# Writing the order of three engines by hand in token passes two and three, and moving the sums of w2 in pass one

## The chip, the core and the metric

The kernel runs on one core of a Trainium2 chip. The metric is the device time of one execution, in microseconds. Five engines take part: TensorE (PE in the profile; its weight loads are PEld), VectorE (DVE), ScalarE (ACT), GpSimd (POOL) and SyncE (SP, which only issues DMAs here). Each engine works through its own queue in order and waits on semaphores for the others.

## What is computed

Block attention, a two-layer MLP, and a mixture of eight experts whose gate is balanced by eight rounds of row and column normalisation. The part that the change touches is the last loop.

```python
# attention (4 batches, 8 heads, 576 tokens, 64 wide) -> x[2304, 512]
h = x @ w_in; x = np.maximum(0.01 * h, h) @ w_out          # 512 -> 2048 -> 512
logits = x @ w_gate                                        # 8 experts
P = np.exp(logits - logits.max())
for _ in range(8):
    P /= P.sum(1, keepdims=True) + 1e-09
    P /= P.sum(0, keepdims=True) + 1e-09
    P *= N / E
out = np.zeros((N, D))
for e in range(E):                                         # E = 8
    h = np.maximum(x @ w1[e], 0.0)                         # 512 -> 1024
    out += P[:, e:e + 1] * (h @ w2[e])                     # 1024 -> 512
```

## The kernel before

All matrix products keep 32-bit accuracy by splitting each operand into a high and a low part, so one product is three matmuls: high by high, high by low, low by high. A split is a ScalarE copy (the high part) and a VectorE subtract (the low part), the helpers `halves`, `parted` and `x_step`.

The expert stage works on three token passes of 768 tokens. In a pass the work is cut into 32 groups of 256 hidden columns (8 experts by 4), which are done in pairs, so a pass has 16 **steps**. A step does `first` 14 times (seven Strassen-Winograd products for each group of the pair; `product` is 6 matmuls of 384 columns), and turns their PSUM results into the four quarters of the hidden layer.

In pass one a step then ends with six `combine` calls (72 matmuls of 512 columns). Pass one also makes the weights' parts: `w2_split` splits a raw w2 tile for this pass; `w2_more` builds four sums of its quarters on GpSimd, in place in the raw tile, splits them (`halves`) and stores the parts in DRAM through the SP queue (`keep_parts`) for the later passes. The high half goes into the tile `wb`, the low half into the tile `tl`, one after the other. `w2_load` then fetches the next raw tile into the same place.

In passes two and three all steps but the last of a pass also use Strassen-Winograd for the second matrix: the hidden quarters are gated by a row of P (`seat["row"]`, fetched by `row_load`), and for each group four sums S1 to S4 are formed on GpSimd. The seven operands S1, S3, A11, A22, S2, A12, S4 are each split by `parted`. Then `seventh(n, j, c)` multiplies operand j of both groups by its w2 part: 6 matmuls of 384 columns for each of two halves c, accumulated over the step's two groups in PSUM and added by VectorE into `seat`. Between the sevenths `first(n + 2, j)` for j below 6 does the first six products of the next step, so a step of these passes begins with eight products in a row (numbers 6 to 13), and then runs seven blocks of two sevenths. That is 14 x 6 + 14 x 6 = 168 matmuls of 384 columns in a step. PSUM gives the sevenths and two of the products four banks in turn (`o_bank`).

TensorE's order is fixed by hand (`in_order`). The order of VectorE, ScalarE, GpSimd and SP is set by a scheduler from its own estimate of times; `behind` and `tc.issue_after` bind single instructions to come later in a queue than others. In the trace most names are those of tiles that were laid out anew for the later passes: `xllate` holds the splits of S1 and S3, `xhlate` those of S2 and S4, `wraw` and `slots` those of A11 and A22, `wa`, `wb`, `slots` those of A12; `places` and `xa` hold quarters and sums, and `xa` also the seats.

These lines of `quarter_late` say which sums are issued when a quarter is done:

```python
sums = {"A22": [("S1", "A21", "A22", ALU.add)],
        "A11": [("S3", "A11", "A21", ALU.subtract), ("S2", "S1", "A11", ALU.subtract)],
        "A12": [("S4", "A12", "S2", ALU.subtract)]}
```

Of the kernel before, what the change touches and what calls it, by code (L numbers as in the profile page):

```python
# [36 lines left out]
def block_attention_mlp_moe(  # L37
# [697 lines left out]
    def w2_more(n):  # L735
        if n >= N0:
            return
        raw = w2_raw.pop(n)
# [4 lines left out]
        nc.gpsimd.tensor_tensor(out=b21, in0=b22, in1=b21, op=ALU.subtract)  # L743
        for part, x in ((0, raw[:, DM:2 * DM]), (1, raw[:, 0:DM])):
# [71 lines left out]
    def x_src(p, k, make):  # L816
# [4 lines left out]
        if make and change:  # L821
            nc.vector.tensor_tensor(out=src, in0=change[0], in1=change[1], op=ALU.subtract)
        return src

    def x_step(p, k, make=True):
        src = x_src(p, k, make)
        hi, lo = (xpart.tile([P, 2, HT], F32R, name=f"x{n}{k}", tag=f"x{n}{k}") for n in "hl")
        nc.scalar.copy(out=hi, in_=src)
        nc.vector.tensor_tensor(out=lo, in0=src, in1=f32(hi), op=ALU.subtract)
        bq[p, k] = (hi, lo)  # L830
# [101 lines left out]

    def keep_late(n, name, k):
        nc.scalar.copy(out=place[k, n % 2], in_=bank[n, name][:, 0:HT])  # L934

    def parted(n, k, x):
        hi, lo = hq[n, k] = slot[k, n % 2]
        nc.scalar.copy(out=hi, in_=x)
        nc.vector.tensor_tensor(out=lo, in0=x, in1=f32(hi), op=ALU.subtract)  # L939

    def quarter_late(n, k, name, add):
        g, x, r = n % 2, bank[n, name][:, 0:HT], ROLE[k]
        q = {j: place[j, g] for j in ("A11", "A12", "A21", "A22", "S1", "S2", "S3", "S4")}
        y = q[r]
        if add:
            nc.vector.tensor_tensor(out=y, in0=x, in1=place[add, g], op=ALU.add)  # L946
            x = y
        nc.vector.scalar_tensor_tensor(  # L948
            out=y, in0=x, scalar=0.0, in1=seat["row"][:, int(k[1]) - 1], op0=ALU.max, op1=ALU.mult
        )  # L950
        sums = {"A22": [("S1", "A21", "A22", ALU.add)],
                "A11": [("S3", "A11", "A21", ALU.subtract), ("S2", "S1", "A11", ALU.subtract)],
                "A12": [("S4", "A12", "S2", ALU.subtract)]}
        if r == "A12":
            parted(n, r, y)
        for to, i0, i1, op in sums.get(r, ()):
            nc.gpsimd.tensor_tensor(out=q[to], in0=q[i0], in1=q[i1], op=op)  # L957
            parted(n, to, q[to])
            if to in ("S1", "S3"):
                parted(n, r, y)  # L960

    def quarter_last(n, k, name, add):
        g, x, r = n % 2, bank[n, name][:, 0:HT], ROLE[k]
        if add:
            c = place[add, g]
            nc.vector.tensor_tensor(out=c, in0=x, in1=c, op=ALU.add)
            x = c
        hi, lo = hq[n, k] = slot["S2" if r == "A21" else r, g]
        nc.scalar.activation(out=hi, in_=x, func=AF.Relu)
        t = nc.vector.scalar_tensor_tensor(out=lo, in0=x, scalar=0.0, in1=f32(hi), op0=ALU.max, op1=ALU.subtract)  # L970
        last_taken[:] = [getattr(t, "ins", t)]
# [5 lines left out]
    def seventh(n, j, c):  # L977
# [10 lines left out]
        if groups[n][1:] == (0, 0):  # L988
            nc.scalar.copy(out=to, in_=o)
        else:  # L990
            nc.vector.tensor_tensor(out=to, in0=o, in1=to, op=ALU.add)  # L991
        return mm

    def join(j):
        if j == 4:
            nc.vector.tensor_tensor(out=seat[6], in0=seat[6], in1=seat[1], op=ALU.add)
            nc.vector.tensor_tensor(out=seat[7], in0=seat[7], in1=seat[6], op=ALU.add)
            nc.gpsimd.tensor_tensor(out=seat[6], in0=seat[6], in1=seat[5], op=ALU.add)
            nc.vector.tensor_tensor(out=seat["row"], in0=seat[7], in1=seat[5], op=ALU.add)
# [299 lines left out]
```

## Time and profile before

| what | value |
|---|---|
| time, median of 3 runs | 2337.99 us (2335.53 to 2339.16) |
| the profiled execution, its own time | 2337.28 us |
| its span, first to last instruction | 2335.5 us |
| PE busy | 2146.5 us (92%) |
| DVE busy | 1586.6 us (68%) |
| ACT busy | 847.2 us (36%) |
| POOL busy | 655.3 us (28%) |
| mean granted TensorE clock | 0.952 of full speed |
| DMA moved | 436.87 MB, 187 GB/s on the mean |

Attention fills the span up to 202 us, the MLP up to 586, pass one up to 1139, pass two up to about 1728, pass three the rest. The shares of busy time are averages over these stages. The chain that ended last, the idle time in front of a group of instructions and the timeline of one step say more.

### The profile page before, as it was taken

How to read it: one execution, taken by the hardware profiler on the slowest of the kernel's cores; microseconds unless marked ns; L12 is line 12 of the kernel's file. 1: busy time of each engine (PE TensorE's matmuls, PEld its weight loads, DVE VectorE, ACT ScalarE, POOL GpSimd, SP SyncE). 2: the span in 40 equal slices, each digit the busy share in tenths (PEclk: the TensorE clock that was granted, in tenths of full speed). 3: DMA queues.
4: the chain of work that ended last, by engine and by line, in shares of the span. 5: the costliest groups of instructions: out<-in, count | busy, mean ns of one | idle time of the engine just before them, and what ended most of it. 6: DMA issues, size and time to landing. Idle time of an engine off the chain costs nothing.

```text
span 2335.5 us, 31639 instructions
## 1 busy us (share of the span) xinstructions
PE 2146.5 (92%) x11196; PEld 1946.8 (83%) x11196; DVE 1586.6 (68%) x2707; ACT 847.2 (36%) x1826; POOL 655.3 (28%) x642
## 2 busy tenths in 40 slices
PE   9999999999999999999798888989898898989888
PEld 6667889888888888888787887878798787878787
DVE  7886656655686777777657667675775667576766
ACT  7775322233444444444332222222333222222222
POOL 2222212210245444444112222131312213131221
PEclk9999999999999999999898989989898988989899
DMA  5551201100578888889665656465665646555562
GB/s 138 122 126 43 64 28 46 46 28 30 210 279 299 294 302 290 301 294 331 235 219 187 221 186 223 174 218 188 224 239 185 224 170 219 191 201 209 186 226 87
DMA packets 235742, 436.87 MB, mean 187 GB/s; under 512 B 77864, under 2 KB 114728, under 8 KB 235328
## 3 DMA queue, kind: packets, MB, share of 16 engines
q1 hardware_dynamic: 234384, 434.56, 54.2%
q8 instruction: 88, 1.44, 0.2%
q14 instruction: 70, 0.57, 0.1%
q10 hardware_dynamic: 1200, 0.30, 0.1%
HBM read 308.82 MB, written 125.95 MB: 186 GB/s over the span
## 4 chain that ended last, share of the span: by engine, by line
PE 80%; DVE 15%; DMA 3%; issue 1%; ACT 0%; POOL 0%; SPq 0%; ACTq 0%; DVEq 0%; POOLq 0%
PE h_ps L842 23%; PE o L985 20%; PE o L1032 11%; PE h_ps L499 9%; PE o L519 8%; PE sc L317 3%; DVE xllate L939 3%; DVE slots L939 3%; DVE wraw L939 2%; PE av L382 2%; PE tr L357 2%; DMA k_0h<-wb 2%; DVE places L948 1%; DVE places L946 1%; DVE xa L948 1%
## 5 line engine op out<-in xcount | busy, mean ns | idle before, releaser
L991 DVE TENSOR_TENSOR xa<-o,xa 128x384 f32<-128x384 f32 x392 | 217.2, 555 | 276.4 <-PE o L985 275.4
L985 PE MATMUL o<-xllate,w2h 128*128 128x384 f32 x480 | 169.4, 419 | 165.0 <-DVE xllate L939 141.4
L957 POOL TENSOR_TENSOR xa<-xa 128x384 f32<-128x384 f32 x90 | 105.9, 1177 | 718.4 <-DVE xa L948 678.5
L985 PEld LDWEIGHTS o<-xllate,w2h 128*128 128x128 f32 x480 | 111.9, 238 | 191.9 <-DVE xllate L939 158.7
L842 PE MATMUL h_ps<-xhS,w1h 128*128 128x384 f32 x768 | 259.0, 337 | 6.7 <-ACT places L934 6.7
L842 PE MATMUL h_ps<-xlS,w1h 128*128 128x384 f32 x768 | 257.9, 336 | 0.0
L842 PE MATMUL h_ps<-xhS,w1l 128*128 128x384 f32 x768 | 257.7, 336 | 0.0
L934 ACT COPY places<-h_ps 128x384 f32<-128x384 f32 x192 | 91.9, 480 | 434.9 <-PE h_ps L842 423.9
L842 PE MATMUL h_ps<-xhA,w1h 128*128 128x384 f32 x448 | 164.5, 367 | 10.2 <-DVE c L859 9.7
L842 PE MATMUL h_ps<-xlA,w1h 128*128 128x384 f32 x448 | 162.1, 362 | 0.0
L842 PE MATMUL h_ps<-xhA,w1l 128*128 128x384 f32 x448 | 160.7, 359 | 0.0
L842 PEld LDWEIGHTS h_ps<-xhS,w1h 128*128 128x128 f32 x768 | 145.2, 189 | 7.0 <-ACT places L934 7.0
L842 PEld LDWEIGHTS h_ps<-xlS,w1h 128*128 128x128 f32 x768 | 145.2, 189 | 0.0
L842 PEld LDWEIGHTS h_ps<-xhS,w1l 128*128 128x128 f32 x768 | 145.2, 189 | 0.0
L1032 PE MATMUL o<-w2h,xhlate 128*128 128x512 f32 x408 | 143.9, 391 | 0.0
L1032 PE MATMUL o<-w2h,xllate 128*128 128x512 f32 x384 | 134.4, 390 | 0.6 <-ACT xllate L865 0.5
L985 PE MATMUL o<-xhlate,w2h 128*128 128x384 f32 x480 | 121.8, 334 | 0.0
L519 PE MATMUL o<-hh,w2h 128*128 128x512 f32 (+1 forms) x320 | 117.7, 368 | 0.0
L519 PE MATMUL o<-hh,w2l 128*128 128x512 f32 (+1 forms) x320 | 117.7, 368 | 0.0
L759 POOL TENSOR_TENSOR wa<-wraw 128x256 f32<-128x256 f32 x32 | 28.2, 881 | 318.2 <-DVE w1l L777 310.6
L507 DVE TENSOR_TENSOR g<-h_ps,g 128x512 f32<-128x512 f32 (+1 forms) x80 | 50.9, 636 | 97.1 <-ACT g L506 96.8
L519 PE MATMUL o<-hl,w2h 128*128 128x512 f32 (+1 forms) x320 | 115.2, 368 | 0.0
(259 smaller groups left out, 5738.2 us busy)
## 6 DMA issues: line engine op xcount, KB each, us to landing
wraw<-in_moe_w_dram SPq DMA_DIRECT2D x64, 512.0 KB, 4.6
w1h<-k_1h SPq DMA_DIRECT2D x64, 512.0 KB, 5.2
w1l<-k_1l SPq DMA_DIRECT2D x64, 512.0 KB, 6.4
w2l<-k_1l SPq DMA_DIRECT2D x60, 512.0 KB, 7.0
w2h<-k_1h SPq DMA_DIRECT2D x60, 512.0 KB, 6.2
w1h<-k_0h SPq DMA_DIRECT2D x64, 384.0 KB, 3.6
w1l<-k_0l SPq DMA_DIRECT2D x64, 384.0 KB, 4.1
w2h<-k_0h SPq DMA_DIRECT2D x60, 384.0 KB, 3.9
```

Source lines behind the costliest of these rows:

```text
L317: nc.tensor.matmul(sc, qbd[p % 2][:, i, :], kT[p % 2][:, lo:hi], start=True, stop=True)
L357: nc.tensor.transpose(tr[:, s].rearrange("p h q -> p (h q)"), ex[p % 2][:, off[i] + c * P:off[i] + (c + 1) * P], ident,)
L499: nc.tensor.matmul(ps[:, 0:n], w[:, c, cols], x, start=c == 0 and s == 0, stop=c == KC - 1 and s == 2,)
L507: nc.vector.tensor_tensor(out=g[:, 0:n], in0=ps[:, 0:n], in1=g[:, 0:n], op=ALU.max)
L519: nc.tensor.matmul(ps[:, 0:n], w[:, cut], h[:, 0:n], start=start and m == 0, stop=stop and m == 2)
L842: mm = nc.tensor.matmul(ps, w[:, c], x[:, c], start=first and c == 0 and s == 0, stop=c == 1 and s == 2, skip_group_check=True,)
L934: nc.scalar.copy(out=place[k, n % 2], in_=bank[n, name][:, 0:HT])
L939: nc.vector.tensor_tensor(out=lo, in0=x, in1=f32(hi), op=ALU.subtract)
L957: nc.gpsimd.tensor_tensor(out=q[to], in0=q[i0], in1=q[i1], op=op)
L985: mm = nc.tensor.matmul(o, a, b, start=i == 0, stop=i == 5)
L991: nc.vector.tensor_tensor(out=to, in0=o, in1=to, op=ALU.add)
L1032: mm = nc.tensor.matmul(o, h, w, start=m == 0, stop=m == 11)
```

## The change

It has two parts. In token passes two and three a new helper `next_on` issues each VectorE, ScalarE and GpSimd instruction behind the last one that it issued on that engine, so the three queues follow the order of the program text, and the text is put in a new order: the sums S1 of both groups come with the last product that they need, then S3, then S2; the splits of S1 and S3 come with products 10 to 13, those of A11 right behind them, and those of A22, S2, A12 and S4 each beside one seventh (`beside_seventh`). The gating of quarter "11" moves beside the first sevenths, and `row_load` behind the first block of sevenths. In pass one `w2_more` is cut in two: the four sums now follow `w2_split` of the same tile, and `w2_away` later splits and stores them, with the low half written over the raw values and the high halves in two tiles, `th` and `wb`. The next raw tile is fetched when `w2_away` has been issued. The last products' inputs of the turn from pass two to three (`x_step`) move behind the first four `combine` calls.

```diff
     def w2_more(n):
-        raw = w2_raw.pop(n)
+        raw = w2_raw[n]
...
         nc.gpsimd.tensor_tensor(out=b21, in0=b22, in1=b21, op=ALU.subtract)
+
+    def w2_away(n):
+        raw = w2_raw.pop(n)
         for part, x in ((0, raw[:, DM:2 * DM]), (1, raw[:, 0:DM])):
-            hi = rawpool.tile([P, DM], F32R, name="wb", tag="wb", bufs=1)
-            lo = mpool.tile([P, DM], F32R, name="tl", tag="tl")
+            pool, tag = ((mpool, "th"), (rawpool, "wb"))[part]
+            hi = pool.tile([P, DM], F32R, name=tag, tag=tag, bufs=1)
+            lo = x.bitcast(F32R)
             halves(hi, lo, x)
             keep_parts(2, n, part, (hi, lo), DM, 0)
...
+    def next_on(f, *a, **k):
+        with ExitStack() as queued:
+            for t in tails.values():
+                queued.enter_context(tc.issue_after(t))
+            ins = f(*a, **k)
+        ins = getattr(ins, "ins", ins)
+        tails[ins.engine] = ins
...
     def quarter_late(n, k, name, add):
...
+        if k == "12":
+            summed(n, "S1")
+        elif k == "21":
+            summed(n, "S3")
+            parted(n, "S1")
+        elif k == "11":
+            parted(n, "S3")
...
+    def beside_seventh(n, j, g):
+        if j == 0:
+            gated(n + g, "11")
+        elif j < 5:
+            k = (None, "A22", "S2", "A12", "S4")[j]
+            parted(n + g, k)
+            if k == "A12":
+                summed(n + g, "S4")
...
-                if m in (3, 9):
-                    w2_more(n + m // 6)
-                    w2_load(n + 2 + m // 6)
+                if n == 0 and m == 4:
+                    w2_more(n + 1)
+                if m in ((1, 3) if n else (2, 8)):
+                    w2_away(n + m // 3 % 2 if n else n + m // 8)
+                    w2_load(n + 2 + (m // 3 % 2 if n else m // 8))
...
         if p and not closing(n):
-            if groups[n + 2][1] != e:
-                row_load(p, e + 1)
+            for k in ("A11", "S2"):
+                for g in range(2):
+                    (parted if k == "A11" else summed)(n + g, k)
             for j in range(len(sevens)):
                 for c in range(2):
                     seventh(n, j, c)
+                    beside_seventh(n, j, c)
...
-            lambda: w2_split(n + 3),
-            lambda: None,
+            lambda: (w2_more(n + 2), w2_split(n + 3)),
+            lambda: w2_more(n + 3),
```

VectorE in a step of pass three, before, from the first of the low parts of this stretch; `xllate` are the low parts of S1 and S3, and the first of the last two is S1 of the second group.

```order
L939 TENSOR_TENSOR slots<-xa_2414,slots 128x384
L948 SCALAR_TENSOR_TENSOR xa_2414<-h_ps,xa_2413 128x384
L939 TENSOR_TENSOR xllate<-xa_2414,xllate 128x384
L939 TENSOR_TENSOR wraw<-places,wraw 128x384
L946 TENSOR_TENSOR places<-o_17122,places 128x384
L939 TENSOR_TENSOR slots<-xa_2414,slots 128x384
L939 TENSOR_TENSOR xllate<-xa_2414,xllate 128x384
L939 TENSOR_TENSOR wraw<-xa_2414,wraw 128x384
L946 TENSOR_TENSOR places<-o_17136,places 128x384
L939 TENSOR_TENSOR xhlate<-places,xhlate 128x384
L948 SCALAR_TENSOR_TENSOR places<-places,xa_2413 128x384
L939 TENSOR_TENSOR xllate<-xa_2414,xllate 128x384 x2
```

The same stretch of VectorE's queue after the change, from the gating of quarter A11 of the first group; all hand-ordered rows carry the line of `next_on`.

```order
L948 SCALAR_TENSOR_TENSOR places<-h_ps,xa_2413 128x384
L948 TENSOR_TENSOR xllate<-xa_2414,xllate 128x384
L948 SCALAR_TENSOR_TENSOR xa_2414<-h_ps,xa_2413 128x384
L948 TENSOR_TENSOR xllate<-xa_2414,xllate 128x384
L948 TENSOR_TENSOR places<-o_16458,places 128x384
L948 TENSOR_TENSOR xllate<-xa_2414,xllate 128x384
L948 TENSOR_TENSOR places<-o_16468,places 128x384
L948 TENSOR_TENSOR xllate<-xa_2414,xllate 128x384
L948 TENSOR_TENSOR wraw<-places,wraw 128x384
L948 TENSOR_TENSOR wraw<-xa_2414,wraw 128x384
```

The low part of S1 of the second group stood eleven instructions behind the first low part of the step, and now stands two behind it.

GpSimd in one step, before: S1, S3, S2 of the first group, then S1, S3, S2 of the second (the row with x2 is S1 and S3), then the two S4.

```order
L957 TENSOR_TENSOR xa_2414<-xa_2414 128x384
L957 TENSOR_TENSOR xa_2414<-places,xa_2414 128x384
L957 TENSOR_TENSOR places<-xa_2414,places 128x384
L957 TENSOR_TENSOR xa_2414<-xa_2414 128x384 x2
L957 TENSOR_TENSOR places<-xa_2414 128x384
L957 TENSOR_TENSOR places<-places 128x384 x2
```

And after:

```order
L948 TENSOR_TENSOR xa_2414<-xa_2414 128x384 x2
L948 TENSOR_TENSOR xa_2414<-places,xa_2414 128x384
L948 TENSOR_TENSOR xa_2414<-xa_2414 128x384
L948 TENSOR_TENSOR places<-xa_2414,places 128x384
L948 TENSOR_TENSOR places<-xa_2414 128x384
L948 TENSOR_TENSOR places<-places 128x384 x2
```

Both S1 now stand first, then both S3, then both S2.

GpSimd at the head of pass one, before: sums of w2 (L740 to L743), and the gate's maximum over partitions (L654, with an ISA row ahead of it and one behind it).

```order
L740 TENSOR_TENSOR wraw<-wraw 128x256
L741 TENSOR_TENSOR wraw<-wraw 128x256
L654 ISA
L654 ISA gall<-gmax 128x1
L742 ISA
L742 TENSOR_TENSOR wraw<-wraw 128x256
L743 TENSOR_TENSOR wraw<-wraw 128x256
```

After:

```order
L740 TENSOR_TENSOR wraw<-wraw 128x256
L654 ISA
L654 ISA gall<-gmax 128x1
L741 ISA
L741 TENSOR_TENSOR wraw<-wraw 128x256
L742 TENSOR_TENSOR wraw<-wraw 128x256
L743 TENSOR_TENSOR wraw<-wraw 128x256
```

Three sums instead of two now stand behind the maximum. ScalarE at the same place, before (L658 is the gate's exponential, L776 the high half of a sum, L865 the relu of a quarter):

```order
L658 ACTIVATE pr<-pr,gneg 128x144
L850 COPY s_5824<-h_ps 128x384
L776 CAST wb<-wraw 128x512
L865 ACTIVATE xhlate<-c_5845 128x384
L865 ACTIVATE xhlate<-c_5865 128x384
L865 ACTIVATE xhlate<-h_ps 128x384
L865 ACTIVATE xllate<-c_5855 128x384
L865 ACTIVATE xllate<-h_ps 128x384
L776 CAST wb<-wraw 128x512
```

After:

```order
L658 ACTIVATE pr<-pr,gneg 128x144
L859 COPY s_5826<-h_ps 128x384
L782 CAST th<-wraw 128x512
L782 CAST wb<-wraw 128x512
L874 ACTIVATE xhlate<-c_5847 128x384
L874 ACTIVATE xhlate<-h_ps 128x384
L874 ACTIVATE xhlate<-c_5867 128x384
```

Both high halves of the tile now stand ahead of the relus; before, the second one stood behind five of them.

SP where pass one ends, before: the stores of the last w2 tile's sums (`k_31`), the stores of the output (L1049), and fetches for pass two (L708).

```order
L703 DMA k_31_0h<-wb 128x512
L1049 DMA out_dram<-xa_2412 128x512
L703 DMA k_31_0l<-tl 128x512
L1049 DMA out_dram<-xa_2412 128x512 x2
L708 DMA w2h<-k_1_0h 128x768
L708 DMA w2l<-k_1_0l 128x768
L708 DMA w2l<-k_1_1l 128x1024
L708 DMA w2h<-k_1_1h 128x1024
L1049 DMA out_dram<-xa_2412 128x512
L703 DMA k_31_1h<-wb 128x512
L703 DMA k_31_1l<-tl 128x512
```

After:

```order
L703 DMA k_31_0h<-th 128x512
L703 DMA k_31_0l<-wraw 128x512
L703 DMA k_31_1h<-wb 128x512
L708 DMA w1h<-k_0_1h 128x1024
L708 DMA w1l<-k_0_1l 128x1024
L703 DMA k_31_1l<-wraw 128x512
```

The last store stood behind all six output stores and now stands ahead of them.

## Rows read from the trace of the kernel before

**Rows 1.** The page: chain that ended last, and the costliest waiting matmul group.
```profile
PE 80%; DVE 15%; DMA 3%; issue 1%; ACT 0%; POOL 0%; SPq 0%; ACTq 0%; DVEq 0%; POOLq 0%
L985 PE MATMUL o<-xllate,w2h 128*128 128x384 f32 x480 | 169.4, 419 | 165.0 <-DVE xllate L939 141.4
```
**Rows 2.** Busy time by stretch, with columns: pass one, then pass two.
```profile
core 0: us, PE busy (x) PEld busy (x) DVE busy (x) ACT busy (x) POOL busy (x), PEclk, DMA share, GB/s
...
728.00:1139.00 411.00, 401.34 (x1994) 359.38 (x1994) 306.44 (x439) 187.46 (x355) 175.94 (x188) 0.99 0.85 305
1139.00:1706.00 567.00, 484.35 (x2534) 470.88 (x2535) 379.88 (x620) 155.10 (x322) 141.48 (x122) 0.91 0.58 201
```
**Rows 3.** Timeline of PE, one step: product 6, first seventh, its last wait.
```profile
1406.40 0.33 PE L842 MATMUL h_ps<-xhS,w1h 128*128 128x384 f32 x1
...
1414.72 0.34 PE L985 MATMUL o<-xllate,w2h 128*128 128x384 f32 x1
...
1421.62 0.69 PE L985 MATMUL o<-xllate,w2h 128*128 128x384 f32 x1 [4.31 <-DVE xllate L939]
```
**Rows 4.** Busy time and clock (third number from the end) in four short stretches.
```profile
1421.60:1426.25 4.65, 4.63 (x15) 4.63 (x15) 4.65 (x8) 1.12 (x3) 2.01 (x2) 0.50 0.21 62
1426.25:1444.00 17.75, 17.75 (x104) 17.75 (x104) 6.85 (x13) 3.29 (x7) 0.00 (x0) 1.00 0.43 148
949.00:953.00 4.00, 2.85 (x17) 2.53 (x16) 3.41 (x7) 2.42 (x6) 0.00 (x0) 1.00 0.77 261
728.00:732.00 4.00, 3.47 (x14) 3.47 (x15) 3.47 (x8) 1.86 (x4) 0.00 (x0) 0.74 0.87 273
```
**Rows 5.** Chain in order of time over one step: start, us, what.
```profile
1411.80 0.56 DVE places L948
...
1421.10 0.48 DVE xllate L939
...
1421.62 2.93 PE o L985 x8
...
1459.18 2.93 PE o L985 x8
```
**Rows 6.** Low parts, sums, high parts: count, durations in ns (min/median/max).
```profile
L939 DVE TENSOR_TENSOR xllate<-xa,xllate x120: 542/722/1346, 1152.2 to 2281.6; 128x384 fp32r<-128x384 f32 x120
...
L957 POOL TENSOR_TENSOR xa<-xa x90: 1008/1197/1326, 1148.9 to 2276.5; 128x384 f32<-128x384 f32 x90
...
L938 ACT CAST xllate<-xa x120: 511/512/516, 1149.9 to 2277.7; 128x384 fp32r<-128x384 f32 x120
```
**Rows 7.** Timeline of POOL and DVE in the same step.
```profile
1411.06 1.02 POOL L957 TENSOR_TENSOR xa<-xa 128x384 f32<-128x384 f32 x1 [22.54 <-DVE xa L948]
...
1412.50 1.20 POOL L957 TENSOR_TENSOR xa<-places,xa 128x384 f32<-128x384 f32 x1 [0.42 <-DVE places L948]
...
1412.74 1.37 DVE L939 TENSOR_TENSOR slots<-xa,slots 128x384 fp32r<-128x384 f32 x1
...
1414.95 2.59 POOL L957 TENSOR_TENSOR xa<-xa 128x384 f32<-128x384 f32 x2
```
**Rows 8.** Timeline of POOL and PE around the gate's maximum.
```profile
622.56 0.38 POOL L654 PARTITION_ALL_REDUCE gall<-gmax  x1 [6.92 <-issue]
...
625.11 0.69 PE L842 MATMUL h_ps<-xhA,w1h 128*128 128x384 f32 x1 [5.24 <-DVE c L859]
...
627.48 0.69 PE L842 MATMUL h_ps<-xhA,w1h 128*128 128x384 f32 x1
...
630.00 0.72 POOL L742 TENSOR_TENSOR wraw<-wraw 128x256 f32<-128x256 f32 x1 [7.06 <-issue]
```
**Rows 9.** Timeline of SP, ACT and PE where pass two begins.
```profile
1131.24 0.52 SPq L703 DMA_DIRECT2D k_1l<-tl  x1
...
1138.65 1.24 ACT L934 COPY places<-h_ps 128x384 f32<-128x384 f32 x3 [10.95 <-DMA k_1l<-tl]
...
1139.18 0.69 PE L842 MATMUL h_ps<-xhS,w1h 128*128 128x384 f32 x1 [6.71 <-ACT places L934]
```

More of the change, by code (lines that the diff above doesn't have):

```diff
@@ L821, in x_src @@
         if make and change:
-            nc.vector.tensor_tensor(out=src, in0=change[0], in1=change[1], op=ALU.subtract)
+            (next_on if tails else lambda f, **k: f(**k))(
+                nc.vector.tensor_tensor, out=src, in0=change[0], in1=change[1], op=ALU.subtract
+            )
         return src
@@ L931, in block_attention_mlp_moe @@
     ROLE = {"21": "A11", "11": "A12", "22": "A21", "12": "A22"}
+    tails = {}
+    def next_on(f, *a, **k):
[5 more added lines that the diff above has]
+        tails[ins.engine] = ins
     def keep_late(n, name, k):
-        nc.scalar.copy(out=place[k, n % 2], in_=bank[n, name][:, 0:HT])
-    def parted(n, k, x):
+        next_on(nc.scalar.copy, out=place[k, n % 2], in_=bank[n, name][:, 0:HT])
@@ L937, in parted, with gated @@
+    def parted(n, k):
         hi, lo = hq[n, k] = slot[k, n % 2]
-        nc.scalar.copy(out=hi, in_=x)
-        nc.vector.tensor_tensor(out=lo, in0=x, in1=f32(hi), op=ALU.subtract)
+        x = place[k, n % 2]
+        next_on(nc.scalar.copy, out=hi, in_=x)
+        next_on(nc.vector.tensor_tensor, out=lo, in0=x, in1=f32(hi), op=ALU.subtract)
+    def gated(n, k, x=None):
+        y = place[ROLE[k], n % 2]
+        next_on(
+            nc.vector.scalar_tensor_tensor, out=y, in0=y if x is None else x, scalar=0.0,
+            in1=seat["row"][:, int(k[1]) - 1], op0=ALU.max, op1=ALU.mult,
+        )
@@ L941, in quarter_late, with summed @@
+    SUMS = {"S1": ("A21", "A22", ALU.add), "S3": ("A11", "A21", ALU.subtract),
+            "S2": ("S1", "A11", ALU.subtract), "S4": ("A12", "S2", ALU.subtract)}
+    def summed(n, k):
+        i0, i1, op = SUMS[k]
+        next_on(
+            nc.gpsimd.tensor_tensor, out=place[k, n % 2], in0=place[i0, n % 2], in1=place[i1, n % 2], op=op
+        )
     def quarter_late(n, k, name, add):
-        g, x, r = n % 2, bank[n, name][:, 0:HT], ROLE[k]
-        q = {j: place[j, g] for j in ("A11", "A12", "A21", "A22", "S1", "S2", "S3", "S4")}
@@ L944, in quarter_late @@
-        y = q[r]
+        x = bank[n, name][:, 0:HT]
         if add:
[L946 to L960, printed above, removed]
+            next_on(
+                nc.vector.tensor_tensor, out=place[ROLE[k], n % 2], in0=x, in1=place[add, n % 2], op=ALU.add
+            )
+            if k != "11":
+                gated(n, k)
+        else:
+            gated(n, k, x)
@@ L1013, in turn_back @@
                 mm = nc.tensor.transpose(o[:, d * HD + c * P:d * HD + (c + 1) * P], x[:, c, cut], ident)
-        nc.scalar.copy(out=xo[0][:, t, :], in_=o)
+        next_on(nc.scalar.copy, out=xo[0][:, t, :], in_=o)
         return mm
@@ L1044, in combine @@
         else:
-            nc.vector.scalar_tensor_tensor(
-                out=a, in0=o, scalar=pr[:, tt, e:e + 1], in1=a, op0=ALU.mult, op1=ALU.add
+            (next_on if p else lambda f, **k: f(**k))(
+                nc.vector.scalar_tensor_tensor, out=a, in0=o, scalar=pr[:, tt, e:e + 1], in1=a,
+                op0=ALU.mult, op1=ALU.add,
             )
@@ L1200, in block_attention_mlp_moe @@
                 in_order(gate_rows)(o_bank, rows_owed.pop(0))
-            if turn and m == (2 if p == 0 else 8):
+            if turn and p == 0 and m == 2:
                 x_step(p + 1, "A11")
@@ L1229, in block_attention_mlp_moe @@
                     join(j)
+                if j == 0 and groups[n + 2][1] != e:
+                    row_load(p, e + 1)
                 if j == 2:
@@ L1251, in block_attention_mlp_moe @@
                 normal(h_bank)
-            behind(more[m])
-            if turn and m < 3:
+            if p == 0:
+                behind(more[m])
+            if turn and p == 0 and m < 3:
                 behind(lambda: x_step(p + 1, terms[m + 1], m == 1))
+            if turn and p and m < 4:
+                x_step(p + 1, terms[m], m == 2)
+                if m == 0:
+                    for k in ("S1", "S3"):
+                        x_src(p + 1, k, True)
         if turn:
```

36 lines of the change are left out of this document (20 added, 16 removed).

## The prediction

> **What bounds the kernel now.** I read the page's chain first: 80% of it lies on PE and 15% on VectorE, and the matmul group with by far the most idle time ahead of it is L985, the sevenths: 165.0 us, of which 141.4 end with VectorE writing `xllate`, the low parts of S1 and S3 [rows 1]. The stretches say where: pass two has PE busy for 484 of 567 us at a granted clock of 0.91, pass one for 401 of 411 at 0.99 [rows 2]. So passes two and three wait, 30 times: two passes by 15 steps that have sevenths, 165.0 / 30 = 5.5 us each.
>
> One step on the timeline: eight products run from 1406.40 to 1414.72, that is 48 matmuls in 8.32 us or 0.1733 us a matmul; then the first seventh (operand S1) starts, stalls, and goes on only at 1421.62, when the low part of S1 of the second group is there [rows 3]. From 1411.80 until then the chain runs through VectorE alone [rows 5]. Its queue is not too long but in a bad order: eleven instructions stand between the first low part and the one that PE waits for, and GpSimd makes S1 of that group as its fourth sum, from 1414.95, though S1 of the first began at 1411.06 [rows 7]. After the stall PE works at a granted clock of 0.50, the lower level of 1.2 GHz, for 4.65 us, and then at 1.00 (2.4 GHz) [rows 4].
>
> The period of a step is 1459.18 - 1421.62 = 37.56 us [rows 5]. Its 168 matmuls at 0.1733 us need 29.1 us. The other 8.4 us are 5.5 idle, 2.3 for the stretch at half clock (half of 4.65) and 0.6 around the restarts.
>
> **Part 1: the steps of passes two and three.** No instruction is added or taken away, and PE's order in a step stays. I walk the new order from t = 0 at the start of the eight products (1.04 us each). The gating of A11 of the first group stands at t = 5.4 in the old trace (1411.80), 0.2 behind the fifth product, and S1 of the first group starts at t = 4.66 [rows 5, 7]; both can't be earlier. What runs beside what matters here: a low part takes 0.542 us at best and 1.346 at worst, a sum 1.008 to 1.326 [rows 6]. The row at 1412.74 shows why: it began during a sum that ended at 1413.70, and ended 0.41 behind it [rows 7]. So I let a VectorE instruction with two SBUF operands end 0.45 behind the sum that runs, and the next sum start when that one has ended. GpSimd then does S1 of group one until t = 5.7; the gating of group two's A22 ends at 6.15; S1 of group two runs to 7.25; the low part of the first S1 ends at 7.7; S3 of group one, held until then, ends at 8.6; the high part (0.51, rows 6) is long there, and the second low part of S1 ends at 9.05. PE has finished the eight products at 8.32 and wants this low part at its fifth matmul of the seventh, at 9.0. The stall is 0.1 to 0.3 us instead of 5.5.
>
> The next needs come the same way: the second low part of S3 at t = 11.9 against 12.3 on PE, the low parts of A11 end at 13.8, and the bank of the first seventh is emptied at 14.35 against 14.75, where the third operand wants it. From there a seventh half with its share of a product gives VectorE 1.56 us for one seat addition and one low part, some 1.1 us; S4's two sums have 4 us of room. Margins of 0.4 us are thin, so I take 0.4 us a step for all stalls: 29.5 us a step, and (37.5 - 29.5) x 30 = **240 us less**. With no stall at all it is 30 x 8.4 = 252.
>
> The Trainium skill, on the page SBUF — State Buffer (section "SBUF: two separate sides"), has a rule that speaks against this order: GpSimd and a VectorE instruction with two SBUF inputs take the shared port pair in turn, and the one that comes second is blocked for the other's whole instruction. The new order sets six sums close together beside six low parts, so by that rule every pair adds up. The row at 1412.74 agrees with it, and the walk above already adds them up; were both to run side by side at their shortest, the low part would be there before 8.3 and the sum would be 12 us lower.
>
> Short waits need not drop the clock: PE was idle for 1.15 of the 4 us from 949 and kept 1.00, while a wait of under 2 us at 728 went with 0.74 [rows 4]. I take no loss of clock.
>
> Covers of the rest. DMA: a step moves 201 GB/s x 37.5 us, some 7.5 MB, so 29.5 us need 256 GB/s; pass one ran at 305 for 411 us [rows 2], so it stays hidden; bounds 0 and, if it got no faster than 240, 2 us a step. `row_load` waits for the gating of quarter 11, at t = 15 in both orders, and SP's queue keeps its order there; nothing. The turn from pass two to three moves `x_step` under six `combine` calls of 2.7 us, with PE busy; -1 to +3 us, I take 0.
>
> **Part 2: pass one.** (a) Where pass two begins, PE is idle for 6.71 us because ScalarE's first write into the newly laid-out `places` waits for the last store of `tl`, issued at 1131.24 and landing 7 us later [rows 9]. That store was late because both high halves went through one tile `wb` and it stood behind six output stores. Now it stands ahead of them and has its own tiles, so it should land before PE needs the place. Gain 6.71 and a spell at the low clock as in rows 4: **9 us**. What is late next there, I see nothing; bounds 0 and 9.
>
> (b) At the head of pass one GpSimd computes the gate's maximum, with gaps of 6.92 us ahead of it and 7.06 us behind it in which it waits for nothing shown [rows 8]. Before, one sum of w2 stood directly behind the second gap for a high half that ScalarE wanted late. Now three do, and ScalarE has both high halves in front of the relus that empty PSUM's quarters. GpSimd goes on at about 629.5, the third sum ends at 631.8, ScalarE's second half at 632.4, VectorE's low half and the next two of its instructions at 634. The product that started at 627.48 [rows 8] waits until then: 6.5 us, and about 1 us of a second spell at half clock. **Cost 7.5 us**, between 0 and 10.
>
> The Trainium skill, page GPSIMD Engine Reference (section "Instruction dispatch"), gives some 6 us for the first call of freshly loaded code. The rows show 6.92 and 7.06; by the page's figure the cost would be an estimated 6.5, one us less.
>
> (c) In the other steps the next raw tile's load now waits for two stores out of the same place, on SP, where later stores queue behind it. The sums come a third of a step earlier in exchange. All of PE's idle time in pass one is 10 us from 728 on [rows 2], so the gain is at most that; a cost of up to the 7 us that a store took to land [rows 9] in a few of the 14 steps is the other end, 20 us. I take 0, as PE's waits there were few.
>
> **Sum**, on the profiled execution (2337.28 us; the span is 1.8 us less, the median 0.7 more): 2337.3 - 240 - 9 + 7.5 = 2095.8; with the 0.7, **2096.5**.
>
> **Rivals.**
>
> *A, the port takes more.* If each low part meets one sum more than in my walk, S1's last comes 1.0 to 1.3 us later, and S3's and the emptied bank are late too by 0.7: some 2 us a step, 60 us: 2156. If the clock falls with it as at 728, another 1 us: 2186. For it: margins of 0.4 us, low parts of 1.346 us. Against: GpSimd has only six sums in this stretch, and they end at t = 13. Chance 0.16.
>
> *B, slower: VectorE becomes the bound.* Place: the blocks of sevenths, where each seat addition now stands in front of a low part in a fixed queue. If every low part there took 1.35 us, a seventh half would cost VectorE 0.56 + 1.35 = 1.9 us against PE's 1.56; 13.8 + 14 x 1.9 = 40.4 us a step, 2.9 more than now: 2337 + 30 x 2.9 = 2424. It decides from 37.5 us, that is 1.7 us a half. Against: only the two S4 sums run there. Chance 0.02.
>
> *C, it does not do what it says.* The order fixes queues, not waits; if PE's stall rests on the first group's chain and not on the order, a step keeps half its idle time and its clock loss: 30 x 4 less, 2217. Against: the low part waited for is named, and its inputs were there at 1416. Chance 0.04.
>
> *D, better.* No stalls, (b) not paid, pass one 6 better: 2337 - 252 - 9 - 6 = 2070. Chance 0.06.
>
> **How the numbers follow.** My forecast, stalls of up to 1 us a step, has 0.72 and reaches from 2078 to 2125 with the bounds of part 2. The range adds most of the lower half of A: **2076 to 2150**, which leaves out C, B, the upper part of A and the best of D, some 0.18. What this kernel's runs can tell from no change is about 0.2%, 5 us. Faster by more: 0.95; within it: 0.02; slower: 0.03.
>
> **What would show it.** The interval from one step's first seventh to the next near 29.5 us; idle time ahead of the sevenths below 30 us in all; a clock of 1.00 in passes two and three; no wait for a store where pass two begins; a wait of about 6 us on PE some 2 us after it resumes behind the gate's maximum. Wrong would be steps over 31 us with PE waiting for low parts or for a bank, a lower clock in spite of short waits, or DMA near its share in pass one.

## The result and the profile after

The changed kernel took **2082.88 us** (median of 4 runs, 2081.79 to 2084.46) against 2337.94 for the kernel before in the same job: a ratio of 0.8911, 95% interval 0.8895 to 0.8926, or 255 us less. The forecast was 2096.5 with a range of 2076 to 2150. Of all executions behind this document one stands apart: one of the five of the kernel with the maximum on PE took 11751 us, where the other four took 2066 to 2069, and nothing here explains it. The profiled execution has a span of 2080.7 us at a mean granted clock of 0.996 (before: 2335.5 at 0.952).

The page of the kernel after, first its chain, then the group of sevenths that stood in [rows 1] with 165.0 us of idle time ahead of it:

```profile
PE 92%; DVE 4%; issue 1%; DMA 1%; POOL 1%; ACT 1%; SPq 0%; DVEq 0%; POOLq 0%; ACTq 0%
L1019 PE MATMUL o<-xllate,w2h 128*128 128x384 f32 x480 | 124.1, 337 | 3.0 <-DVE xllate L948 2.9
```

VectorE's share of the chain fell from 15% to 4%, the idle time of the sevenths from 165.0 to 3.0 us. The mean of one matmul there fell from 419 to 337 ns: the clock came back with the waits.

Busy time by stretch after, to be read against [rows 2]: the head of pass one, the rest of pass one, most of pass two, most of pass three. The third number from the end is the granted clock.

```profile
586.00:728.00 142.00, 128.66 (x668) 118.08 (x668) 102.58 (x209) 59.96 (x114) 56.12 (x59) 0.94 0.67 244
728.00:1139.00 411.00, 409.94 (x2073) 371.50 (x2073) 320.96 (x443) 194.67 (x363) 180.79 (x191) 1.00 0.87 312
1146.00:1580.00 434.00, 433.90 (x2505) 432.50 (x2504) 357.23 (x613) 143.41 (x314) 139.54 (x119) 1.00 0.74 261
1615.00:2050.00 435.00, 433.52 (x2497) 431.86 (x2496) 360.27 (x617) 143.86 (x314) 143.03 (x122) 1.00 0.72 253
```

In passes two and three PE has little idle time left (0.1 of 434 us and 1.5 of 435), at a granted clock of 1.00. DMA moves 261 and 253 GB/s there, where [rows 2] had 201, and PE does not wait for it.

One step of pass two, on three engines. First PE, where the eight products of this step begin, and the first seventh of this step and of the next:

```profile
1340.79 0.33 PE L851 MATMUL h_ps<-xhS,w1h 128*128 128x384 f32 x1
...
1349.11 0.51 PE L1019 MATMUL o<-xllate,w2h 128*128 128x384 f32 x2
1349.46 0.33 PE L1019 MATMUL o<-xllate,w2l 128*128 128x384 f32 x1
...
1378.27 0.51 PE L1019 MATMUL o<-xllate,w2h 128*128 128x384 f32 x2
```

GpSimd and VectorE around that point:

```profile
1345.43 1.02 POOL L948 TENSOR_TENSOR xa<-xa 128x384 f32<-128x384 f32 x1 [11.08 <-DVE xa L948]
1346.94 1.01 POOL L948 TENSOR_TENSOR xa<-xa 128x384 f32<-128x384 f32 x1 [0.49 <-DVE xa L948]
1347.91 1.34 POOL L948 TENSOR_TENSOR xa<-places,xa 128x384 f32<-128x384 f32 x1
1349.20 1.34 POOL L948 TENSOR_TENSOR xa<-xa 128x384 f32<-128x384 f32 x1
1350.50 1.33 POOL L948 TENSOR_TENSOR places<-xa,places 128x384 f32<-128x384 f32 x1
...
1347.25 1.11 DVE L948 TENSOR_TENSOR xllate<-xa,xllate 128x384 fp32r<-128x384 f32 x1
...
1348.76 0.91 DVE L948 TENSOR_TENSOR xllate<-xa,xllate 128x384 fp32r<-128x384 f32 x1
...
1350.06 0.90 DVE L948 TENSOR_TENSOR xllate<-xa,xllate 128x384 fp32r<-128x384 f32 x1
...
1351.35 0.90 DVE L948 TENSOR_TENSOR xllate<-xa,xllate 128x384 fp32r<-128x384 f32 x1
...
1353.46 0.54 DVE L948 TENSOR_TENSOR wraw<-xa,wraw 128x384 fp32r<-128x384 f32 x1
```

The step is 29.16 us long (1378.27 - 1349.11), where [rows 5] had 37.56. The low part of S1 of the second group is the row at 1348.76: it ends at 1349.67. PE began the seventh at 1349.11, needs that part at its fifth matmul, some 0.7 us later, and no wait is listed: the margin is about 0.1 us. Each of these low parts ends 0.4 us behind a sum (1348.76 + 0.91 against 1347.91 + 1.34; the next two likewise against sums that end at 1350.54 and 1351.83).

The head of pass one, where [rows 8] had PE waiting once, now shows it waiting twice. GpSimd, ScalarE, then PE:

```profile
622.01 0.38 POOL L654 PARTITION_ALL_REDUCE gall<-gmax  x1 [6.32 <-issue]
629.26 0.71 POOL L741 TENSOR_TENSOR wraw<-wraw 128x256 f32<-128x256 f32 x1 [6.87 <-issue]
...
630.01 0.62 ACT L782 CAST th<-wraw 128x512 fp32r<-128x512 f32 x1 [6.62 <-POOL wraw L741]
632.12 0.62 ACT L782 CAST wb<-wraw 128x512 fp32r<-128x512 f32 x1 [1.49 <-POOL wraw L743]
632.65 0.52 ACT L874 ACTIVATE xhlate<-c 128x384 fp32r<-128x384 f32 x1
...
624.74 0.69 PE L851 MATMUL h_ps<-xhA,w1h 128*128 128x384 f32 x1 [4.61 <-DVE c L868]
634.92 0.69 PE L851 MATMUL h_ps<-xhA,w1h 128*128 128x384 f32 x1 [7.89 <-DVE c L868]
```

Where pass two begins, PE's 6.71 us of [rows 9] are gone. The store of a low part that was issued last and held the layout up is now issued 18 us earlier, ahead of the output stores:

```profile
1113.02 0.32 SPq L703 DMA_DIRECT2D k_1l<-wraw  x1
...
1116.08 0.34 SPq L1093 DMA_DIRECT2D out_dram<-xa  x1
```

### The profile page after: what moved, and what is told of

Same layout as the page of the kernel before. It is cut to its first block, busy times and chain, and to the rows that moved or that the text cites. A ratio compares the mean times of both kernels' runs of the same rounds, so it can differ in the third digit from the quotient of the medians.

```text
span 2080.7 us, 31734 instructions
## 1 busy us (share of the span) xinstructions
PE 2056.3 (99%) x11196; PEld 1883.0 (90%) x11196; DVE 1567.5 (75%) x2707; ACT 836.7 (40%) x1826; POOL 660.7 (32%) x642
## 4 chain that ended last, share of the span: by engine, by line
PE 92%; DVE 4%; issue 1%; DMA 1%; POOL 1%; ACT 1%; SPq 0%; DVEq 0%; POOLq 0%; ACTq 0%
PE h_ps L851 27%; PE o L1019 21%; PE o L1075 13%; PE o L519 9%; PE h_ps L499 9%; PE sc L317 4%; PE o L851 3%; PE tr L357 2%; PE av L382 2%; DVE xa L948 1%; PE qm L291 0%; DVE w1l L783 0%; DMA k_0h<-th 0%; PE km L297 0%; PE av L379 0%
## 5 line engine op out<-in xcount | busy, mean ns | idle before, releaser
L948 ACT CAST xllate<-xa 128x384 fp32r<-128x384 f32 x120 | 61.6, 514 | 280.4 <-POOL xa L948 280.4
L851 PE MATMUL h_ps<-xhA,w1h 128*128 128x384 f32 x448 | 152.4, 340 | 14.1 <-DVE c L868 12.9
L851 PE MATMUL h_ps<-xhA,w1l 128*128 128x384 f32 x448 | 150.9, 337 | 0.0
L851 PE MATMUL h_ps<-xlA,w1h 128*128 128x384 f32 x448 | 150.9, 337 | 0.0
L948 POOL TENSOR_TENSOR places<-places 128x384 f32<-128x384 f32 x60 | 61.0, 1017 | 251.3 <-DVE wa L948 234.6
L1019 PE MATMUL o<-xllate,w2h 128*128 128x384 f32 x480 | 124.1, 337 | 3.0 <-DVE xllate L948 2.9
```

The lines of the kernel that those rows point to most:

```text
L851: mm = nc.tensor.matmul(ps, w[:, c], x[:, c], start=first and c == 0 and s == 0, stop=c == 1 and s == 2, skip_group_check=True,)
L948: ins = f(*a, **k)
L1019: mm = nc.tensor.matmul(o, a, b, start=i == 0, stop=i == 5)
```

## The experiments

All are timed against the kernel before in their own job (medians 2335.7 for the first four, 2337.5 for the two that bind copies in the scheduler, 2336.8 for the other four).

### Each part alone

The changed kernel with the old pass one:

```diff
-            pool, tag = ((mpool, "th"), (rawpool, "wb"))[part]
-            hi = pool.tile([P, DM], F32R, name=tag, tag=tag, bufs=1)
-            lo = x.bitcast(F32R)
+            hi = rawpool.tile([P, DM], F32R, name="wb", tag="wb", bufs=1)
+            lo = mpool.tile([P, DM], F32R, name="tl", tag="tl")
...
-            lambda: (w2_more(n + 2), w2_split(n + 3)),
-            lambda: w2_more(n + 3),
+            lambda: w2_split(n + 3),
+            lambda: None,
```

> The changed kernel with pass one as it was before: both high halves through one tile, low halves in a tile of their own, the sums of w2 right ahead of their split. Only the order of passes two and three is new. The steps are 29.15 us apart in the trace of the changed kernel, against 37.5 before: 30 x 8.4 = 252 us. The forecast's part (a) says that PE still waits some 7 us where pass two begins (with a spell at the lower clock, 9 us together), so the gain of pass two and three stands alone: 2338 - 252 = 2086 us, within 4. Rival: the end of pass one has been mended by the new order of the steps and not by the tiles; then no wait stands there and it gives 2077. At the head of pass one the product behind the gate's maximum should start as before, 2.4 us behind the one ahead of it and not 10.

Measured: **2092.46 us** (2090.51 to 2093.65), 243 less than before. The steps are 29.15 us apart, and the wait at the start of pass two stands, so the change of pass one had mended it and not the order of the steps. PE there, then ScalarE:

```profile
1137.44 0.69 PE L845 MATMUL h_ps<-xhS,w1h 128*128 128x384 f32 x1 [6.56 <-ACT places L942]
...
1136.90 1.24 ACT L942 COPY places<-h_ps 128x384 f32<-128x384 f32 x3 [11.12 <-DMA k_1l<-tl]
```

The expectation was 6 us too low: it took 37.5 and 29.15 as the periods throughout. In the changed kernel's trace the first step of each of the two passes takes 31.2 us and not 29.15, and the stretch from the last block of sevenths to the next pass or to PE's last matmul won 7.2 and 8.0 us and not 8.4.

The kernel before with the new pass one, passes two and three untouched (the edit is the rest of the diff shown ahead):

> The kernel before with pass one of the changed kernel alone: sums of w2 behind their split, low parts in the raw tile, two tiles for the high halves; passes two and three as before. By the forecast: -9 at the start of pass two, +7.5 behind the gate's maximum, other steps 0: 2336.5 us. By what the two traces show of pass one (the combine block of the first step 8.3 us later, that of the last step 1.65 us earlier, so some 10 us won over 15 steps): 2338 - 9 + 7.5 - 10 = 2326.5. The two are told apart at 2331. Steps of passes two and three should stay 37.5 us apart; sevenths idle about 165 us.

Measured: **2326.01 us** (2324.92 to 2330.12), 9.7 less; ratio 0.9963, interval 0.9949 to 0.9977. The sevenths wait as before (165.1 us). The two parts add up: 243.2 + 9.7 = 252.9 against 255 for both.

### What in the order of a step makes the gain

The changed kernel with one split put later:

```diff
-            parted(n, "S1")
+            if n % 2 == 0:
+                parted(n, "S1")
...
                     (parted if k == "A11" else summed)(n + g, k)
+                if k == "A11":
+                    parted(n + 1, "S1")
```

> The changed kernel with one pair of instructions put elsewhere in each step: the split of S1 of the second group (ScalarE's copy, VectorE's low part) stands behind the splits of A11 and of S3, where it came late before too. No instruction more or less. If the place of this low part in VectorE's fixed queue is what the 5.5 us of idle time and the clock loss were: by the walk it ends at t = 13.4 instead of 8.9, PE wants it at 9.0, so 4 to 4.5 us idle a step, and some 2 us for a stretch at the lower clock behind it; 30 x 6.3 = 190, so 2083 + 190 = 2273 us (2225 if the clock holds). Rival: what ended the waits is that sums and gatings got closer together, and the place of this one matters little: under 2110.

Measured: **2276.88 us**, 194 more than the changed kernel, or 6.5 us a step, from the place of two instructions. PE in one step, and the clock in the stretches behind its second wait:

```profile
1362.90 0.44 PE L1020 MATMUL o<-xllate,w2h 128*128 128x384 f32 x1 [2.26 <-ACT xllate L948]
1365.01 0.69 PE L1020 MATMUL o<-xllate,w2h 128*128 128x384 f32 x1 [1.68 <-DVE xllate L948]
...
1365.00:1367.00 2.00, 1.99 (x6) 1.99 (x7) 0.94 (x2) 0.00 (x0) 0.00 (x0) 0.50 0.67 274
1367.00:1369.60 2.60, 2.60 (x9) 2.60 (x9) 1.10 (x3) 0.00 (x0) 0.00 (x0) 0.50 0.02 6
```

PE is idle for 3.9 us, and then works for at least 4.6 us at the lower clock, 1.2 GHz, which costs half of that, 2.3: the two components of the old loss, 5.5 and 2.3 + 0.6, in a similar proportion. So the walk's two claims hold: PE waits on the place of this split in a fixed queue (2.26 us for its high part on ScalarE, 1.68 more for its low part on VectorE; the run moved both together), and the wait draws a spell at half clock behind it.

The changed kernel with GpSimd's six sums in group order again:

```diff
-        if k == "12":
+        if k == "12" and n % 2 == 0:
             summed(n, "S1")
         elif k == "21":
+            if n % 2:
+                summed(n, "S1")
             summed(n, "S3")
+            summed(n, "S2")
             parted(n, "S1")
...
-            for k in ("A11", "S2"):
-                for g in range(2):
-                    (parted if k == "A11" else summed)(n + g, k)
+            for g in range(2):
+                parted(n + g, "A11")
```

> The changed kernel with GpSimd's six sums of a step in group order: S1, S3, S2 of the first group, then S1, S3, S2 of the second, in place of S1, S1, S3, S3, S2, S2. VectorE's and ScalarE's order stays. The second S1 then starts two sums later, at t = 8.6 or so in place of 5.7, ends at 9.9, and its high and low part follow by 11.3, against 9.0 at which PE wants it: 2.3 us idle a step, 30 x 2.3 = 69 us, and up to 30 x 1.2 = 36 for clock: 2152 to 2188 us. Rival: GpSimd's order matters little, as VectorE's queue alone set the old wait: under 2100.

Measured: **2178.81 us**, 96 more, or 3.2 us a step. PE waits 1.39 + 0.51 us in each step, where 2.3 were worked out; the longer wait is for ScalarE's high part, which waits for GpSimd's sum. So both queues had to be put in order, VectorE's and GpSimd's. The rest is 1.3 us a step. The steps of this kernel are 31.6 and 33.1 us long in turn, against 29.15: about 0.5 us is lost around the two waits in every step, and in every second one another 1.6 to the clock, 0.8 on the mean. Two neighbouring steps of this kernel with the same two waits (PE's timeline), and the clock behind each pair:

```profile
1340.07 0.44 PE L1022 MATMUL o<-xllate,w2h 128*128 128x384 f32 x1 [1.39 <-ACT xllate L948]
1341.02 0.44 PE L1022 MATMUL o<-xllate,w2h 128*128 128x384 f32 x1 [0.51 <-DVE xllate L948]
1373.22 0.44 PE L1022 MATMUL o<-xllate,w2h 128*128 128x384 f32 x1 [1.39 <-ACT xllate L948]
1374.17 0.44 PE L1022 MATMUL o<-xllate,w2h 128*128 128x384 f32 x1 [0.51 <-DVE xllate L948]
...
1341.50:1344.00 2.50, 2.50 (x11) 2.50 (x10) 2.50 (x5) 0.42 (x2) 0.33 (x1) 0.59 0.86 342
1375.00:1377.00 2.00, 2.00 (x13) 2.00 (x12) 2.00 (x5) 0.13 (x2) 0.00 (x0) 1.00 1.00 408
```

### What in pass one makes the ten microseconds

The changed kernel with one tile for both high halves:

```diff
-            pool, tag = ((mpool, "th"), (rawpool, "wb"))[part]
+            pool, tag = rawpool, "wb"
```

> The changed kernel with both high halves of a w2 matrix through one tile again; sums still behind the split, low parts still in the raw tile. The second half's copy on ScalarE must then wait for the first half's store to land. If the second tile is what the steps of pass one gained from (before, ScalarE waited 29 us in all for stores out of that tile), most of the 10 us won there go: 2083 + 6 to 10 = 2089 to 2093, with ScalarE waiting for the high half's store again. Rival: the gain comes from the earlier sums and from the low parts' own place, and ScalarE's waits were hidden: 2081 to 2085.

Measured: **2104.96 us** (2104.37 to 2108.04), 22 more than the changed kernel, where 6 to 10 were expected, and 12.5 more than with the old pass one (2092.46). ScalarE's waits for DMAs from 728 us to 1150, here:

```profile
ACT wb L782 <- DMA k_0h<-wb: 47.7, 24, 8.7
ACT w2h L129 <- DMA wraw<-in_moe_w_dram: 19.2, 11, 4.4
```

and in the changed kernel:

```profile
ACT th L782 <- DMA k_0h<-th: 2.9, 4, 1.4
```

So the second tile removes the waits for stores. With one tile the rest of the new pass one makes things worse than they were: raw tiles then land late for the split of w2 (19.2 us, where the old pass one has 1.0). The low parts in the raw tile, which hold it until they are stored, are the likely reason; no run has them alone. Pass one's steps, taken from PE's timeline as the distance from one block of `combine` to the next, are 31.0 to 35.0 us here, 31.3 with some of 32.8 and more in the kernel before, and 30.95 in the changed kernel from the sixth on, but for one. At the start of pass two the wait is back:

```profile
1153.87 0.69 PE L851 MATMUL h_ps<-xhS,w1h 128*128 128x384 f32 x1 [7.40 <-ACT places L948]
```

How the old tile cost time is to be seen in the kernel before, in a step of 32.8 us. ScalarE's copy waits for the store out of `wb`, the relu behind it is late, and PE's product waits for that relu:

```profile
1050.01 0.62 ACT L776 CAST wb<-wraw 128x512 fp32r<-128x512 f32 x1 [3.41 <-DMA k_0h<-wb]
1050.53 0.52 ACT L865 ACTIVATE xllate<-c 128x384 fp32r<-128x384 f32 x1
...
1050.18 0.40 PE L1032 MATMUL o<-w2h,xhlate 128*128 128x512 f32 x1
1051.10 0.50 PE L1032 MATMUL o<-w2h,xllate 128*128 128x512 f32 x1 [0.52 <-ACT xllate L865]
```

The idle column says 0.52 us, but the two matmuls begin 0.92 us apart, where neighbours are 0.23 apart: the wait cost 0.69. A wait of under 0.2 us isn't listed at all, since a matmul's shown end reaches into the next one.

The low halves had a store to wait for too, since `tl` was a single tile as well, and from there the way to PE leads over VectorE. PE's longest listed wait of these steps in the kernel before:

```profile
726.38 0.69 DVE L777 TENSOR_TENSOR tl<-wraw,wb 128x512 fp32r<-128x512 f32 x1 [2.57 <-DMA k_0l<-tl]
727.46 1.01 DVE L859 TENSOR_TENSOR c<-h_ps,s 128x384 f32<-128x384 f32 x2
...
728.53 0.45 PE L842 MATMUL h_ps<-xhA,w1h 128*128 128x384 f32 x1 [1.79 <-DVE c L859]
```

Of the waits that are listed for PE between the first and the last `combine` block, 4.4 us are for `c` and 0.5 for a relu. No run has two high tiles with the old `tl`, so how much of the gain is the high halves' and how much the low halves' stays open.

The changed kernel with the four sums back in their old place:

```diff
...
+                    w2_more(n + m // 3 % 2 if n else n + m // 8)
                     w2_away(n + m // 3 % 2 if n else n + m // 8)
...
-            lambda: (w2_more(n + 2), w2_split(n + 3)),
-            lambda: w2_more(n + 3),
+            lambda: w2_split(n + 3),
+            lambda: None,
```

> The changed kernel with the three sums of w2 moved from behind their split to right ahead of the next one, a third of a step later, as before; tiles stay as in the changed kernel. Two things hang on it. At the head of pass one ScalarE's and VectorE's halves that wait for GpSimd behind the gate's maximum: if the place of the sums makes that wait, it shrinks to the old one, 7.4 us less. In the other steps: if the earlier sums are what the steps won by, some 10 us are lost. Forecast by both: 2083 - 7.4 + 5 to 10 = 2081 to 2086. Rival 1: the steps' gain came from the tiles alone: 2075. Rival 2: the wait at the head stays (it is GpSimd's gap and not the sums): 2088 to 2093.

Measured: **2082.19 us**, no difference. This was an empty experiment, and that is its result: in pass one a scheduler sets the queues, and the instructions of all five engines come out in the same order as in the changed kernel. Where the sums are written has no effect. What is left of the pass-one part are the tiles, and the earlier place of `w2_away` in the later steps, which no run varied alone.

### The wait behind the gate's maximum

One call moved four products later (from m = 8 to 12), to take the copies that wait for GpSimd out of the way:

```diff
-                if m in ((1, 3) if n else (2, 8)):
+                if m in ((1, 3) if n else (2, 12)):
...
```

> The changed kernel with one call put elsewhere, once in the kernel: in the first step of pass one the copies and low halves of the second w2 matrix, and the load behind them, come four m later, so that nothing in ScalarE's and VectorE's queues waits for GpSimd's sums behind the gate's maximum. If that queue order is the wait of 7.4 us on PE there: 2083 - 7.4 = 2075.5. Rival: PE waits for the gate's maximum itself, or the later load and stores cost as much further on: 2081 to 2085.

Measured: **2084.31 us**, no difference, for the same reason: no engine's order changed. So the next two bind the copies in the scheduler, behind the relus of the ninth product and, with the m = 12 above, of the thirteenth:

```diff
-                    w2_away(n + m // 3 % 2 if n else n + m // 8)
+                    (w2_away if n or m == 2 else lambda j: behind(lambda: w2_away(j)))(n + m // 3 % 2 if n else n + m // 8)
```

> The changed kernel with the copies and low halves of the second w2 matrix held back in the first step of pass one: the scheduler may put them only behind the relus of the quarter that is then the last one taken. On ScalarE two relus now stand ahead of the two copies that wait for GpSimd's sums, where all stood behind them. (Moving the call alone, four products later, left every engine's order as it was; this one changes it.) Theory: PE's wait of 7.9 us is the first quarters' relus, queued behind these copies; with two ahead, PE's product starts at once and the wait shrinks or moves to the third relu: 2083 - 4 to 7.4 = 2075.5 to 2079. Rival: PE waits for GpSimd in another way (through the buffers that the copies free): 2081 to 2085.

Measured: **2076.49 us** (2075.11 to 2080.80). PE's second wait went from 7.89 to 2.19 us.

> The same with the two copies and low halves held back behind the relus of the thirteenth product, so that seven relus stand ahead of them on ScalarE. Theory: nothing that empties a PSUM bank waits for GpSimd's sums any more, PE's wait of 7.9 us at the head of pass one is gone, the other (4.6, for the maximum itself) stays: 2083 - 7.4 = 2075.5. If the copies come so late that the stores and the next raw tile's load are late in turn, some of it is given back in the next step: up to 2080. Rival: as in the kernel above, 2081 to 2085.

Measured: **2074.11 us** (2073.89 to 2075.86), 8.8 less than the changed kernel. PE's waits in this kernel, summed over the run, have one wait left on `c`, the one for the maximum itself:

```profile
PE h_ps L851 <- DVE c L868: 5.0, 1, 5.0
```

Last, the maximum over partitions without GpSimd:

```diff
-        nc.gpsimd.partition_all_reduce(st["gall"], st["gmax"], P, bass.bass_isa.ReduceOp.max)
+    def gate_row(bank):
+        ps = bank()
+        mm = nc.tensor.transpose(ps[0:1, 0:P], st["gmax"], ident)
+        nc.vector.tensor_reduce(out=st["gall"][0:1, :], in_=ps[0:1, 0:P], axis=AX.X, op=ALU.max)
+        return mm
+    def gate_all(bank):
+        ps = cs_ps[1] = bank()
+        return nc.tensor.matmul(ps[:, 0:1], ones[0:1, :], st["gall"][0:1, :], start=True, stop=True)
...
```

> The changed kernel with the maximum over the partitions of the gate's values taken without GpSimd's all-reduce: a transpose of one column on PE, a maximum on VectorE, and a matmul of one row that hands it to all partitions. GpSimd then has no gap ahead of that operation and none behind it (6.3 and 6.9 us in the trace of the changed kernel). If those two gaps are what PE's two waits at the head of pass one rest on (4.6 and 7.9 us, with spells at the lower clock behind them, some 15 us together): 2083 - 15 = 2068, less about 1 us for the two small PE operations: 2069. Rival: the gaps come with the sums of w2 anyway (whatever GpSimd does first at this place has a gap ahead of it): 2076 to 2083.

Measured: **2067.73 us**, ratio 0.8845, interval 0.8833 to 0.8857: 15 less than the changed kernel, where 14 were expected, and the best of all. GpSimd's four sums at this place, and the new operations on PE and VectorE:

```profile
615.14 0.74 POOL L749 TENSOR_TENSOR wraw<-wraw 128x256 f32<-128x256 f32 x1 [13.19 <-PE o L622]
615.96 0.73 POOL L750 TENSOR_TENSOR wraw<-wraw 128x256 f32<-128x256 f32 x1
616.77 0.73 POOL L751 TENSOR_TENSOR wraw<-wraw 128x256 f32<-128x256 f32 x1
617.59 0.73 POOL L752 TENSOR_TENSOR wraw<-wraw 128x256 f32<-128x256 f32 x1
...
615.99 0.27 PE L657 MATMUL o<-ident,gmax 128*1 128x128 f32 x1
...
616.30 0.28 DVE L658 TENSOR_REDUCE gall<-o 1x1 f32<-1x128 f32 x1 [0.75 <-PE o L657]
```

The sums run back to back: no gap of 6 to 7 us stands between them. The rival, that GpSimd's first operation at this place has a gap whatever it is, falls. PE is then busy for 140.20 of the 142 us from 586, where the changed kernel had 128.66.

## Why the prediction was right, and where it was off

**The bound and the steps (part 1).** Right, and for its reason: the place of one split and the order of the sums, as the two experiments on the order show. The walk came close at each point. It is compared here in its own clock, with t = 0 at 1340.79, where PE's eight products begin:

| event | walk | measured |
|---|---|---|
| second low part of S1 ends | 9.05 | 8.88 |
| second low part of S3 ends | 11.9 | 11.46 |
| low parts of A11 end | 13.8 | 13.21 |

The term that was mis-sized is the 0.4 us a step that it set aside for stalls: the only listed ones are in the first step of each pass (2.9 us in all). From the first seventh of pass two to the start of PE's last matmul, 1178.8 us became 933.1: 245.7 us less, or 8.2 us a step, where the sum had 8.0 and 240. It isn't the full 252, since the first and the last step of each pass won less. No loss of clock: right for this kernel, though the reason, that short waits need not drop the clock, holds only sometimes, as the reordered sums showed. Two slips of the prediction here had no weight: ten instructions and not eleven stand between the two low parts, and S3 of group one was given 0.9 us, less than the shortest sum of [rows 6].

The walk's 0.45 us between the end of a sum and that of the low part beside it held too: the low parts of the step shown that ran beside a sum ended 0.4 us behind it and took 0.90 us and more instead of 0.54. The Trainium skill, page SBUF — State Buffer (section "SBUF: two separate sides"), says that GpSimd and a VectorE instruction with two SBUF inputs take the shared pair in turn for a whole instruction; the trace agrees. Rival A (one sum more ahead of each low part) did not come about: sums and low parts alternate one by one. Rival B has no trace either: VectorE is busy for 357 of 434 us in pass two, and C's waits are gone. Of rival D's three conditions two came true: no stalls, and a better pass one; (b) was paid.

**(a) The start of pass two.** Forecast -9. From the two traces, the first seventh of pass two moved forward by 9.4 us, of which 1.65 was already there at the last `combine` block of pass one: -7.8. Each kernel with a single high tile has the wait (6.56, 7.40 us), each with two has not.

**(b) The head of pass one.** Forecast +7.5; the first `combine` block stood 8.3 us later. The cause is as told, and was shown: with seven relus ahead of the two copies the time falls by 8.8 us. What the prediction didn't say is why the sums slid behind the maximum at all: the scheduler placed one sum and not two ahead of it, and moving the sums in the text does not alter that; what in the change made it do so stays open. The prediction also counted one sum behind the gap in the kernel before; there were two, L742 and L743.

**(c) The other steps of pass one.** Forecast 0, measured -10: from 8.3 us behind at the first `combine` block to 1.65 ahead at the last. This is the step that failed. It took the idle time that the trace lists (10 us, of which 6.7 are the start of pass two and belong to (a)) as the most that could be won, and called PE's waits few; that the gain came out at 10 too is chance. The listed idle time leaves out what a wait costs around it and all waits under 0.2 us, and the cause was in sight: ScalarE waited 29.4 us for stores out of `wb`, 19 times, with relus queued behind it, and VectorE's low halves waited for those copies, or for stores out of `tl`, with `c` queued behind them. That the second high tile acts is shown; the share of `tl` is not. The cost that it feared, loads that wait on SP for two stores, is there (46.5 us in 12 waits of SP's queue) and hidden.

The sum: -245.7 - 7.8 + 8.3 - 10 = -255.2. Against the forecast's -241.5, the steps were off by 6 and pass one's steps by 10, and both erred towards slow; (a) and (b) erred by about 1 us each the other way.

## What to carry to other kernels

Where one engine's queue is in a fixed order, write down for each result when its reader wants it, and walk producers and their producers in that order: two instructions in the wrong place cost 194 us here, another order of the six sums 96. Ahead of a scheduler, moving text may do nothing: see first that an engine's order really changes; what acts there is a second tile, a binding, or an operation less. And a copy into a single tile that waits for its store stands in front of everything behind it on its engine, whether or not the trace lists idle time for it.

## What the runs showed of the hardware

The granted clock did not answer the same waits in the same way: behind 1.39 + 0.51 us of waiting it was 0.59 in one step and 1.00 in the next of the same run. Behind 2.26 + 1.68 us it was 0.50 for at least 4.6 us.

GpSimd's all-reduce cost far more than its 0.38 us: a gap of 5.9 to 6.9 us ahead of it and of 6.7 to 7.6 behind it, in which the trace shows nothing waited for, in every kernel that has it, and none at all in the one that doesn't. The Trainium skill, page GPSIMD Engine Reference (section "Instruction dispatch"), puts the first call of freshly loaded code at some 6 us; the gap ahead agrees. The second gap, behind the operation, is as long, and here it cost more: PE waited 4.61 us on the first and 7.89 on what was queued behind the second.
